# Spreading a finished batch's routing work over the next head pairs, in a block attention and top-1 expert kernel

## The chip, the cores and the metric

The kernel runs on one core of one Trainium2 chip. The metric is the device time in microseconds (us) from start to end of one execution, taken as the median over several runs. A profile is one execution of its own, with its own time.

## What is computed

Eight batches of eight heads with 576 positions and 64 dimensions go through attention with a block mask (blocks of 64 positions; a query sees its own block and the earlier ones). The rows of the result (4608 tokens of 512) then go through one of eight experts each, with two gates:

```python
scores = scale * np.matmul(q, k.transpose(0, 1, 3, 2))
scores = np.where(block_i >= block_j, scores, -1e9)
attn = softmax(scores)                       # over the keys
x = (attn @ v).transpose(0, 2, 1, 3).reshape(B * S, H * D)

e_idx = argmax(x @ w_gate)                   # one expert for each token
gate_w = softmax(x @ w_gate)[e_idx]
eom = sigmoid(x @ w_output_gate)
for e in range(E):
    out[e_idx == e] = gate_w * eom[:, e] * (relu(x @ w1[e]) @ w2[e])
```

## The kernel before, in words

The engines are called PE (TensorE), DVE (VectorE), ACT (ScalarE), POOL (GpSimd) and SP (SyncE, which issues most of the DMAs).

**Attention.** The outer loop runs over 32 pairs of heads, numbered 0 to 31, four pairs to a batch. The queries of a pair are cut into four tiles of 128 rows and a last one of 64. Pair p is worked on in three turns of the loop: in turn p its scores, in turn p+1 its flips, in turn p+2 its values. So one turn (`attend`) holds the scores of a pair, the flips of the pair before and the values of the pair before that.

- *Scores* (`softmax`) are a generator of four steps, here S1 to S4. Each fills a tile of `ps_s`, which is two banks of PSUM and of which there are two, so S3 takes the banks of S1, S4 those of S2, and the next pair's S1 and S2 those of S3 and S4. DVE takes the negated maxima (`nmx`, L374), ACT the exponentials (`pt`, L367; for S4 `plast`, L418). S1 does tiles 0 and 1, S2 tile 2, S3 tile 3, S4 the last. Ahead of S4 DVE also builds `qlast` (L393).
- *Flips* (`flip`), F1 to F4, transpose the exponentials on PE. F1 to F3 use `ps_f`, of which there is one (two banks), and ACT and DVE each copy one half out into `pT` (L445). F4 uses a bank of `ps_t` (L467, copied by ACT, L468).
- *Values* (`values`), V1 and V2, multiply the flipped exponentials with v (L481, L494) into a bank of `ps_t`. The result is copied to `xT` by ACT (L488, the first 512 positions) and by DVE (L498, the last 64).

`ps_t` has two banks, handed out in turn. Whoever asks for one waits until the tile that had it two requests earlier has been read.

**A finished batch's rest** is a generator, `finish_batch`, that is appended to the list `later` at the end of the turn that holds the values of the batch's last pair. In the attend loop each `t` is a tick, which moves every generator in `later` on by one yield; there are four ticks to a pair. The generator does, in this order: the sums of the last tile (`sumL`, a product on PE and two small copies), the reciprocals `rec`, the logits of both gates from `xT` in a part of 512 and one of 64 columns (L545, copied to `lgT`), their transposes (L561, L571) with a DVE product each into `lh`, a reduction of `lh` to the logits `L` (L577), the routing on small tiles (on POOL for the first five batches, on DVE for the others), a product that ranks the tokens of each expert (`pr`, L645 to L651), and five scatters of the tokens' slots into a table in DRAM. In between, `rows(t)` transposes one tile of `xT` back (four transposes, L517), DVE multiplies it with `rec` (L520), and one tick later `store` sends it to `x_d` in DRAM (L532).

**Order.** PE runs in the order in which the program issues its instructions within a turn. The other engines' queues are ordered by a planner of its own when the kernel is built, by costs and priorities; an instruction in `issue_after` stays behind a given one, and the maxima, for one, have a raised priority. The order of a turn is written in one string in `attend`. A dot in it calls `others`, which feeds SP and POOL: POOL splits q and k into two halves of 16 bits, SP turns them (`qk`, L164, a DMA transpose; from pair 8 on two pairs ahead, before that one), and SP loads q, k and v of later batches.

**The experts.** At pair 30 `load_first` is appended to `later`. In its first tick it finds the fullest expert, reads the table (`fetch_ids`, L889), gathers the first tokens from `x_d` (`xg`, L900) and loads that expert's first weights; from its sixth tick on it converts them. After pair 31 one more turn runs without scores, in which `stage_x` transposes the first gathered tokens (L999). Then the expert stage runs over 22 steps to the end.

Of the kernel before, what the change touches and what calls it, by code (L numbers as in the profile page):

```python
# [10 lines left out]
F32 = mybir.dt.float32  # L11
I32 = mybir.dt.int32
U32 = mybir.dt.uint32
AF = mybir.ActivationFunctionType
# [6 lines left out]
P = 128  # L21
# [5 lines left out]
def block_attention_top1_moe(  # L27
# [11 lines left out]
    nc = tc.nc  # L39
    B, H, S, D = q.shape  # L40
    NTOK, DM = out.shape
    E, _, FF = w1.shape
    NP = H // 2
# [4 lines left out]
    LAST = NT - 1  # L48
    S0 = P * LAST
# [23 lines left out]
    ps_t = tc.alloc_tile_pool(name="ps_t", bufs=2, space=PSUM)  # L73
    ps_f = tc.alloc_tile_pool(name="ps_f", bufs=1, space=PSUM)
    sbx = ctx.enter_context(tc.tile_pool(name="sbx", bufs=2))
# [62 lines left out]
    def queued():  # L138
        return tc.issue_after(last_turn[0].ins) if last_turn[0] else nullcontext()
# [57 lines left out]
    with tc.high_priority(offset=3000):  # L197
        ident16 = const.tile([P, P], F16, name="ident16")
        make_identity(nc, ident16)
        ident = const.tile([P, P], F32, name="ident")  # L200
# [301 lines left out]

    def finish_batch(b, sums, sumL, xT):

        pm = ps_t.tile([P, 512], F32, name="ps_t")
        nc.tensor.matmul(pm[0:64, 0:NP], ident[:, 64:128], sumL, start=True, stop=True)
        sv = sums[0:64, LAST].rearrange("p (g a) -> p a g", a=2)
        nc.scalar.copy(sv[:, 0], sumL[0:64])
        nc.vector.tensor_copy(sv[:, 1], pm[0:64, 0:NP])
        rec = small.tile([P, NT, H], F32, name="rec")  # L510

        def rows(t):

            r = ROWS[t]
            pm = ps_t.tile([P, 512], F32, name="ps_t")
            for g in range(NP):
                nc.tensor.transpose(pm[0:r, P * g:P * g + P], xT[:, g, Q0[t]:Q0[t] + r], ident)  # L517
            xn = sbx.tile([P, DM], F32, name="xn", bufs=NT)
            with tc.high_priority(offset=5):
                last_row[0] = nc.vector.tensor_tensor(  # L520
                    xn[0:r].rearrange("p (h d) -> p h d", d=D), pm[0:r].rearrange("p (h d) -> p h d", d=D),
                    rec[0:r, t].unsqueeze(2).broadcast_to([r, H, D]), ALU.mult,
                )
            held.append((x_d[b * S + Q0[t]:b * S + Q0[t] + r, :], xn[0:r]))
            if rush:
                store()

        def store():

            while held:  # L530
                with queued() if not rush else nullcontext():
                    nc.sync.dma_start(*held.pop())  # L532

        held, rush = [], b == B - 1
        if not rush:
            yield
        nc.scalar.activation(rec, sums, AF.Copy, bias=1e-9)
        if rush:
            nc.vector.reciprocal(rec, rec)

        lgT = sbx.tile([P, S], F32, name="lgT", bufs=1)
        for c0, c1 in ((0, 512), (512, 576)):
            pm = ps_t.tile([P, 512], F32, name="ps_t")
            for g in range(NP):
                nc.tensor.matmul(  # L545
                    pm[32 * g:32 * g + 32, 0:c1 - c0], wg_bd[:, g, :], xT[:, g, c0:c1],
                    start=True, stop=True, tile_position=(0, 32 * g),
                )
            nc.scalar.copy(lgT[:, c0:c1], pm[:, 0:c1 - c0])
            if not rush:  # L550
                yield
                if c0 == 0:
                    nc.vector.reciprocal(rec, rec)
        yield
        if not rush:
            rows(LAST)
            yield
            store()
        pm = ps_t.tile([P, 512], F32, name="ps_t")
        for t in range(LAST):  # L560
            nc.tensor.transpose(pm[:, P * t:P * t + P], lgT[:, Q0[t]:Q0[t] + P], ident)  # L561
# [8 lines left out]
        pm = ps_t.tile([P, 512], F32, name="ps_t")  # L570
# [14 lines left out]
        def on_pool(*ops):  # L585

            for op, args in ops:
                with behind() if slow else nullcontext():
                    ins = getattr(eng, op)(*args)
                if slow:  # L590
                    last_pool[0] = ins

        def after(last):
            return tc.issue_after(last[0].ins) if slow else nullcontext()

        def part(n):

            for x in range(n if slow else 0):
                yield

        def part_rows(t):

            if slow:
                rows(t)
                yield
                store()
# [3 lines left out]
        er = small.tile([P, NT], F32, name="er")  # L610
        oh = small.tile([P, NT, E], F16, name="oh")
        z = small.tile([P, NT, E], F32, name="z")
        yield from part(1)
        yield from part_rows(0)
        on_pool(
            ("tensor_tensor", (d, lg, mxb, ALU.subtract)),
            ("tensor_scalar", (eq, d, 0.0, None, ALU.is_equal)),
            ("tensor_tensor", (eq, eq, erev.unsqueeze(1).broadcast_to([P, NT, E]), ALU.mult)),
        )
        yield from part_rows(1)  # L620
        yield from part_rows(2)
        with after(last_max):
            nc.vector.tensor_reduce(er, eq, AX.X, ALU.max)
        yield from part_rows(3)
        erb = er.unsqueeze(2).broadcast_to([P, NT, E])
        on_pool(
            ("tensor_tensor", (eq, erb, erev.unsqueeze(1).broadcast_to([P, NT, E]), ALU.subtract)),
# [4 lines left out]
        if slow:  # L632
            with after(last_exp):
                nc.scalar.activation(d, d, AF.Exp)
        yield from part(2)
        if not slow:
            yield
            if not rush:
                for t in range(LAST):
                    rows(t)  # L640
                    yield
                    store()
# [28 lines left out]
        with after(last_max):  # L671
            nc.vector.tensor_reduce(zs, z, AX.X, ALU.add)
        yield from part(1)
        with after(last_exp):
            last_gate[0] = nc.scalar.activation(zs, zs, AF.Exp, scale=-1.0)
        yield from part(1)
# [464 lines left out]
    def attend(soft, extra=None):  # L1141

        nxt, flipped, valued = [], iter(()), iter(())
        if flips:
            hp, b, probs, sums, xT, vab = flips.pop()
            pT = sb.tile([P, 2, NPT], F32, name="pT")
            nxt = [(hp, b, pT, vab, sums, xT)]
            flipped = flip(probs, pT)
        if prods:
            hp, b, pT, vab, sums, xT = prods.pop()  # L1150
            valued = values(hp, pT, *vab, xT)
        else:
            hp = None
        def tick():
            for g in list(later):
                if next(g, later) is later:
                    later.remove(g)

        turns = iter(range(4))
        with tc.manual_schedule(engines=ENG):  # L1160
            for x in "S.F.SVFSV.FttSFtt.":
                if x == "S":
                    step(soft)
                elif x == "V":
                    step(valued)
                elif x == "F":
                    step(flipped)
                elif x == "t":
                    tick()
                elif extra is not None:  # L1170
                    extra(next(turns))

        if hp == NP - 1:
            later.append(finish_batch(b, *sums, xT))
        prods.extend(nxt)
# [4 lines left out]
    for p in range(NPR):  # L1180
        b, hp = divmod(p, NP)
        if hp == 0:
            sums = small.tile([P, NT, H], F32, name="sums", bufs=3), small.tile([P, NP], F32, name="sumL", bufs=3)
# [67 lines left out]
    ps_t = ctx.enter_context(tc.tile_pool(name="ps_y", bufs=4, space=PSUM, reuse_waits="tile"))  # L1251
    attend(iter(()), both_x)
    hp, b, pT, vab, sums, xT = prods.pop()
    ended = values(hp, pT, *vab, xT)
    rush = finish_batch(b, *sums, xT)
# [133 lines left out]
```

## Time and profile before

| | us |
|---|---|
| median of 3 runs | 743.06 |
| lowest and highest run | 740.52 to 744.53 |
| the profiled execution | 739.44 |
| its span, from the first to the last instruction | 737.8 |
| PE busy (share of the span) | 694.3 (94%) |
| DVE busy | 543.7 (74%) |
| ACT busy | 498.5 (68%) |
| POOL busy | 322.2 (44%) |

Busy times are those of the one profiled execution. Attention runs from the start to about 320 us, the experts from there to the end. Matmuls are pipelined and their ends are modelled, so a busy PE is not PE at its peak. A wait is the idle time of an engine just before an instruction, put down to the engine or DMA whose signal came last.

### The profile page before, as it was taken

Reading aid. Unit: us, or ns where it says so; the run is one execution under the profiler, and the core shown is the slowest. Engines: PE = TensorE matmul, PEld = TensorE weight load, DVE = VectorE, ACT = ScalarE, POOL = GpSimd, SP = SyncE. Lnnn points to the kernel's source line nnn. Section 1 sums busy time; section 2 is a strip of 40 time slices with the busy share of each in tenths; the row PEclk is TensorE's granted clock in tenths of the full one; section 3 lists DMA queues with packets and bytes.
Section 4 is the critical chain, followed back from the end, with each engine's and each line's share of the span. In section 5 each row is a group of like instructions: output and inputs, shape, how many; then the busy total and the mean of one; then the engine's idle time right before and its main releaser. Section 6 shows DMA issues by size and latency. Waiting matters only on the chain. (4 is left out here: it accounts for less than half of the span.)

```text
span 737.8 us, 21153 instructions
## 1 busy us (share of the span) xinstructions
PE 694.3 (94%) x8298; PEld 492.7 (67%) x8298; DVE 543.7 (74%) x948; ACT 498.5 (68%) x1097; POOL 322.2 (44%) x407
## 2 busy tenths in 40 slices
PE   5899899999999898989989999999999999999994
PEld 4666666767677676657568666876577676767861
DVE  6887878888797879798757558955588667858830
ACT  5888777878687886873357558765576577658630
POOL 4365378685758583246366523422233124211011
PEclk9999999999999999999999999999999999999998
DMA  7699897999989898176645796987999999686601
GB/s 199 143 198 224 181 219 132 205 151 177 203 181 178 155 152 173 55 270 137 186 143 131 221 281 190 298 88 255 250 306 361 290 325 342 220 232 191 240 31 46
DMA packets 235997, 146.85 MB, mean 199 GB/s; under 512 B 187120, under 2 KB 203568, under 8 KB 235888
## 3 DMA queue, kind: packets, MB, share of 16 engines
q1 hardware_dynamic: 227136, 125.85, 70.2%
q0 software_dynamic: 8208, 19.29, 8.5%
q8 instruction: 67, 1.10, 0.7%
q14 instruction: 42, 0.34, 0.1%
q10 hardware_dynamic: 544, 0.26, 0.1%
HBM read 126.43 MB, written 19.34 MB: 198 GB/s over the span
## 5 line engine op out<-in xcount | busy, mean ns | idle before, releaser
L1055 PEld LDWEIGHTS <-w1b 128*128 128x128 f16 (+1 forms) x2208 | 176.3, 98 | 26.3 <-issue 4.9
L1055 PE MATMUL ps_s<-xt,w1b 128*128 128x256 f16 (+5 forms) x1920 | 175.3, 253 | 0.3 <-DVE w1b L933 0.2
L1090 PE MATMUL ps_t<-w2b,hh 128*128 128x512 f16 (+1 forms) x560 | 166.5, 379 | 0.0
L933 DVE TENSOR_TENSOR w2b<-w2f,w2b 128x1024 bf16<-128x1024 f32 x80 | 92.9, 1220 | 88.1 <-ACT w2b L931 88.1
L374 DVE TENSOR_REDUCE nmx<-ps_s 128x1 f32<-128x512 f32 (+4 forms) x224 | 130.0, 617 | 11.4 <-PE ps_s L363 6.8
L367 ACT ACTIVATE pt<-ps_s,nmx 128x256 f32<-128x256 f32 (+3 forms) x256 | 131.9, 534 | 8.8 <-DVE nmx L374 8.7
L1098 POOL DMA_INDIRECT out_dram<-ys,ids x38 | 45.3, 1192 | 174.6 <-ACT ys L1097 95.9
L1090 PE MATMUL ps_t<-w2b,hl 128*128 128x512 f16 x280 | 106.1, 379 | 0.0
L1097 ACT ACTIVATE ys<-ps_t,ids 128x512 f32<-128x512 f32 (+1 forms) x38 | 26.0, 685 | 103.7 <-PE ps_t L1090 77.2
L933 DVE TENSOR_TENSOR w1b<-w1f,w1b 128x1024 bf16<-128x1024 f32 x80 | 93.1, 1218 | 3.8 <-ACT w1b L931 3.6
L1090 PEld LDWEIGHTS <-hh 128*128 128x128 f16 x560 | 54.3, 98 | 61.7
L355 PE MATMUL ps_s<-qk 64*128 64x256 f16 (+1 forms) x1152 | 73.8, 252 | 11.5 <-ACT plast L418 3.7
L445 DVE COPY pT<-ps_f 128x512 f32<-128x512 f32 x93 | 63.8, 686 | 28.0 <-PE ps_f L442 25.9
L481 PE MATMUL ps_t<-pT,vv 128*64 128x256 f32 (+3 forms) x512 | 83.0, 445 | 0.4 <-DVE lh L572 0.4
L931 ACT CAST w1b<-w1f 128x1024 f16<-128x1024 f32 x80 | 78.5, 1045 | 7.0 <-DMA w1f<-in_moe_w_dram 6.9
L931 ACT CAST w2b<-w2f 128x1024 f16<-128x1024 f32 x80 | 77.9, 1043 | 1.0 <-DMA w2f<-in_moe_w_dram 0.7
L900 POOL DMA_INDIRECT xg<-x_d,ids x38 | 62.5, 1646 | 32.8 <-DMA ids<-tab_d 7.0
L355 PEld LDWEIGHTS <-qk 64*128 64x128 f16 x1152 | 49.9, 94 | 23.5 <-issue 14.9
L445 ACT COPY pT<-ps_f 128x512 f32<-128x512 f32 x93 | 55.3, 595 | 10.0 <-PE ps_f L442 8.9
L442 PEld LDWEIGHTS ps_f<-ident,pt 64*128 64x128 f32 x1116 | 42.2, 138 | 25.6 <-issue 12.3
L1063 ACT ACTIVATE hh<-ps_s 128x1024 f16<-128x1024 f32 (+2 forms) x46 | 38.9, 845 | 29.5 <-PE ps_s L1055 27.5
L442 PE MATMUL ps_f<-ident,pt 64*128 64x64 f32 x1116 | 54.1, 229 | 4.2 <-DVE pT L445 2.3
(220 smaller groups left out, 1029.3 us busy)
## 6 DMA issues: line engine op xcount, KB each, us to landing
w1f<-in_moe_w_dram SPq DMA_DIRECT2D x80, 512.0 KB
w2f<-in_moe_w_dram SPq DMA_DIRECT2D x80, 512.0 KB
vv<-in_v_dram SPq DMA_DIRECT2D x64, 128.0 KB
x_d<-xn SPq DMA_DIRECT2D x32, 256.0 KB
natk<-in_k_dram SPq DMA_DIRECT2D x14, 512.0 KB
natq<-in_q_dram SPq DMA_DIRECT2D x28, 256.0 KB
hh<-in_moe_w_dram SPq DMA_DIRECT2D x4, 512.0 KB
hl<-in_moe_w_dram SPq DMA_DIRECT2D x4, 512.0 KB
```

What stands on the lines that cost most here:

```text
L355: nc.tensor.matmul(ps[:, ab, c:c + m], qk[rows, cq, P * t:P * t + P], cols(qk[rows, ck], x, kind), start=(i == 0), stop=(i == 2 and c + m ...
L367: last_exp[0] = nc.scalar.activation(probs[t][:, ab], ps[:, ab, c0:c0 + n], AF.Exp, bias=nmx[:, t, ab:ab + 1], accum_out=sums[:, t, 2 * hp ...
L374: last_max[0] = nc.vector.tensor_reduce(o, x, AX.X, ALU.max, negate=True)
L442: nc.tensor.transpose(ps[:, h, 64 * i:64 * i + 64], src[rows], ident[rows, rows])
L445: copy(to[:, h], ps[:, h].rearrange("p (s c) -> p s c", c=P))
L481: nc.tensor.matmul(pa[o, P * j:S0].rearrange("p (t h n) -> p t h n", h=2, n=64), vv[:, j, a0 + ab], pT[:, :, x:x + P * m].rearrange("p h ( ...
L900: nc.gpsimd.indirect_dma_start(out=xg[i % NXG][:, h], out_offset=None, in_=x_d[0:nx, :], in_offset=IOA(ap=ids[i][:, h, 0:1].bitcast(U32), ...
L931: nc.scalar.copy(hi, src)
L933: eng.tensor_tensor(lo, src, hi, ALU.subtract)
L1055: nc.tensor.matmul(ph[:, f4].rearrange("p (h n) -> p h n", n=w), wv[:, cc, f, :], xv[:, cc, :, 0:w], start=(k == 0), stop=(k == 3 * KD - 1))
L1090: nc.tensor.matmul(py, hv[:, f, h], wv[:, f, :], start=(k == 0), stop=(k == 3 * KF - 1))
L1098: nc.gpsimd.indirect_dma_start(out=out, out_offset=IOA(ap=ids[i][0:r, h, 0:1].bitcast(U32), axis=0), in_=ys[0:r], in_offset=None, bounds_c ...
```

## The change

Three things change; what is computed stays the same.

- The order of a turn: before `S.F.SVFSV.FttSFtt.`, after `S.tF.VSFSV.FttSFt.`. V1 moves from behind S2 to ahead of it. Of the four ticks of a pair, the one at the very end moves to the place behind S1, ahead of F1; two stay between F3 and S4, one behind F4.
- The short part of the logits (64 columns) is taken in the first tick, in the same PSUM tile as the sums; the long part in the second.
- The tiles of `rows` are laid out differently over the ticks. For the first five batches: before, the last tile in tick 5, then 0 to 3 in ticks 8 to 11, the ranking in tick 14 and the scatters from tick 20 on; after, the transposes of the logits in ticks 5 and 6, the last tile and tile 0 in ticks 9 and 10, tiles 1 and 2 in ticks 13 and 14, the ranking in tick 16, tile 3 in tick 17, and the scatters from tick 23 on. The later batches (but the very last) take the last tile behind the routing instead of ahead of it.

```diff
@@ finish_batch @@
-        pm = ps_t.tile([P, 512], F32, name="ps_t")
-        nc.tensor.matmul(pm[0:64, 0:NP], ident[:, 64:128], sumL, start=True, stop=True)
-        sv = sums[0:64, LAST].rearrange("p (g a) -> p a g", a=2)
-        nc.scalar.copy(sv[:, 0], sumL[0:64])
-        nc.vector.tensor_copy(sv[:, 1], pm[0:64, 0:NP])
         rec = small.tile([P, NT, H], F32, name="rec")
...
-        held, rush = [], b == B - 1
-        if not rush:
-            yield
-        nc.scalar.activation(rec, sums, AF.Copy, bias=1e-9)
-        if rush:
-            nc.vector.reciprocal(rec, rec)
-
         lgT = sbx.tile([P, S], F32, name="lgT", bufs=1)
-        for c0, c1 in ((0, 512), (512, 576)):
-            pm = ps_t.tile([P, 512], F32, name="ps_t")
+
+        def logits(c0, c1, pm):
             for g in range(NP):
                 nc.tensor.matmul(
                     pm[32 * g:32 * g + 32, 0:c1 - c0], wg_bd[:, g, :], xT[:, g, c0:c1],
                     start=True, stop=True, tile_position=(0, 32 * g),
                 )
             nc.scalar.copy(lgT[:, c0:c1], pm[:, 0:c1 - c0])
-            if not rush:
-                yield
-                if c0 == 0:
-                    nc.vector.reciprocal(rec, rec)
-        yield
-        if not rush:
-            rows(LAST)
+
+        held, rush = [], b == B - 1
+        pm = ps_t.tile([P, 512], F32, name="ps_t")
+        nc.tensor.matmul(pm[0:64, P:P + NP], ident[:, 64:128], sumL, start=True, stop=True)
+        sv = sums[0:64, LAST].rearrange("p (g a) -> p a g", a=2)
+        nc.scalar.copy(sv[:, 0], sumL[0:64])
+        nc.vector.tensor_copy(sv[:, 1], pm[0:64, P:P + NP])
+        if rush:
+            nc.scalar.activation(rec, sums, AF.Copy, bias=1e-9)
+            nc.vector.reciprocal(rec, rec)
+            logits(0, S0, ps_t.tile([P, 512], F32, name="ps_t"))
+            logits(S0, S, ps_t.tile([P, 512], F32, name="ps_t"))
             yield
-            store()
+        else:
+            logits(S0, S, pm)
+            yield
+            nc.scalar.activation(rec, sums, AF.Copy, bias=1e-9)
+            logits(0, S0, ps_t.tile([P, 512], F32, name="ps_t"))
+            yield
+            nc.vector.reciprocal(rec, rec)
+            yield
+            yield
...
-        yield from part(1)
-        yield from part_rows(0)
+        yield from part(3)
         on_pool(
...
-        yield from part_rows(1)
-        yield from part_rows(2)
+        yield from part_rows(LAST)
+        yield from part_rows(0)
         with after(last_max):
             nc.vector.tensor_reduce(er, eq, AX.X, ALU.max)
-        yield from part_rows(3)
+        yield from part(1)
...
-        yield from part(2)
+        yield from part(1)
+        yield from part_rows(1)
+        yield from part_rows(2)
+        yield from part(1)
         if not slow:
             yield
             if not rush:
-                for t in range(LAST):
+                for t in (LAST, *range(LAST)):
...
         yield from part(1)
+        yield from part_rows(3)
         with after(last_exp):
             last_gate[0] = nc.scalar.activation(zs, zs, AF.Exp, scale=-1.0)
@@ attend @@
-            for x in "S.F.SVFSV.FttSFtt.":
+            for x in "S.tF.VSFSV.FttSFt.":
```

## Rows read from the trace of the kernel before

**Rows 1.** Busy time by stretch: start, length, engines, granted clock, DMA share, GB/s.

```profile
100.00:200.00 100.00, 95.36 (x1549) 68.93 (x1547) 82.47 (x179) 79.68 (x251) 75.10 (x114) 1.00 0.97 179
200.00:300.00 100.00, 93.82 (x1538) 68.52 (x1539) 85.32 (x194) 78.17 (x248) 62.25 (x94) 1.00 0.83 161
500.00:600.00 100.00, 100.00 (x887) 69.37 (x885) 66.98 (x66) 64.91 (x79) 26.79 (x24) 1.00 0.99 299
```

**Rows 2.** Waits of PE, 30 to 380 us: total, times, longest us.

```profile
PE ps_s L355 <- ACT plast L418: 3.7, 9, 0.7
PE ps_t L999 <- DMA xg<-x_d,ids: 2.6, 1, 2.6
PE ps_s L355 <- DMA qk<-sp: 2.5, 2, 1.4
PE ps_f L442 <- DVE pT L445: 2.3, 5, 0.5
...
PE ps_s L355 <- ACT pt L367: 1.8, 7, 0.3
...
PE ps_t L545 <- DVE xT L498: 1.1, 1, 1.1
PE ps_t L517 <- ACT xT L488: 0.7, 1, 0.7
PE ps_t L571 <- DVE lh L562: 0.6, 1, 0.6
PE ps_t L545 <- DVE sums L509: 0.5, 1, 0.5
PE ps_f L442 <- DVE d L589: 0.5, 1, 0.5
```

**Rows 3.** Timeline of PE: start, us, line, what, count, [idle before].

```profile
42.79 0.92 PE L412 MATMUL ps_s<-qk,qlast 128*128 128x256 f16 x9
...
45.42 0.67 PE L355 MATMUL ps_s<-qk 64*128 64x256 f16 x12 [0.28 <-ACT plast L418]
...
46.05 1.73 PE L481 MATMUL ps_t<-pT,vv 128*64 128x512 f32 x8
47.71 0.58 PE L442 MATMUL ps_f<-ident,pt 64*128 64x64 f32 x12
...
51.05 0.92 PE L412 MATMUL ps_s<-qk,qlast 128*128 128x256 f16 x9
...
110.86 0.92 PE L412 MATMUL ps_s<-qk,qlast 128*128 128x256 f16 x9
...
149.22 0.92 PE L412 MATMUL ps_s<-qk,qlast 128*128 128x256 f16 x9
```

**Rows 4.** Timeline of DVE, 122 to 126 us.

```profile
122.46 0.69 DVE L520 TENSOR_TENSOR xn<-ps_t,rec 128x512 f32<-128x512 f32 x1 [0.36 <-PE ps_t L517]
123.07 1.23 DVE L577 TENSOR_REDUCE L<-lh 128x80 f32<-128x640 f32 x1
...
125.25 0.69 DVE L445 COPY pT<-ps_f 128x512 f32<-128x512 f32 x1
```

**Rows 5.** Timelines of PE's weight loads (PEld) and of SP around waits for qk.

```profile
92.38 0.11 PEld L355 LDWEIGHTS <-qk 64*128 64x128 f16 x3 [1.95 <-DMA qk<-sp]
...
257.99 0.17 PEld L355 LDWEIGHTS <-qk 64*128 64x128 f16 x6 [1.59 <-DMA qk<-sp]
...
247.75 0.57 SPq L532 DMA_DIRECT2D x_d<-xn  x1
...
249.97 4.45 SPq L164 DMA_TRANSPOSE qk<-sp  x1
```

**Rows 6.** Timelines of PE, DVE and POOL at the first table read.

```profile
305.81 0.18 PE L719 MATMUL ps_t<-run_cnt,ones 128*128 128x8 f16 x1
...
306.38 0.15 DVE L721 COPY cnt<-ps_t 128x8 f32<-128x8 f32 x1
...
310.74 0.78 POOL L889 DMA_DIRECT2D ids<-tab_d  x1 [10.30 <-DVE nmx L374]
```

## Prediction

> **What bounds the kernel now.** I read the engine shares first, then the busy time by stretch, then who waits for whom, then the timelines of TensorE (PE), VectorE (DVE), ScalarE (ACT) and SyncE (SP). By stretch, PE is busy for 95.4% and 93.8% of the attention loop (100 to 200 and 200 to 300 us) and for 100% of the expert stage, at a granted clock of 1.00 in all three [rows 1]. So the expert stage starts and ends as much earlier as attention does, and what the change can win is PE's idle time in attention.
>
> That time is small and named. Between 30 and 380 us PE waits 3.7 us (9 times) for ACT's exponential of the last tile (plast), 2.3 us for the DVE half of a flip's copy and 0.5 us more under another DVE name, 1.8 us for the exponentials pt, 2.5 us for turned q and k (qk), 2.6 us for the first gathered tokens (xg), and four times 0.5 to 1.1 us for a bank of ps_t [rows 2].
>
> A pair of heads without any rest of a batch in it takes 51.05 - 42.79 = 8.26 us from one S4 to the next, of which 0.28 us is a wait for plast [rows 3]: 7.98 us of PE work. DVE and ACT are busy for 82.5% and 79.7% from 100 to 200 us [rows 1], rest included, so they have room on average. The waits come from work that arrives in a lump.
>
> **The change, part by part.** The sum is made against the profiled execution, 739.4 us (span 737.8), which is 3.6 us under the median of 743.06; I carry the difference over to the median.
>
> *V1 ahead of S2.* S2 fills the pair of ps_s banks that the S4 before it filled, so it waits for the exponential of plast. Before, F4, two ticks, S1 and F1 lie between them; now V1 does too. V1 takes 47.71 - 46.05 = 1.66 us [rows 3], and no wait for plast is above 0.7 us [rows 2]. All 3.7 us should go. What it costs: this 1.66 us no longer lies between S2 and F2, S3, F3. I laid such a pair out by hand with the start-to-start times of the 20 rows from 42.79 to 51.05 [rows 3]: S1 at 0, F1 0.56, V1 1.24, S2 2.90, F2 3.53, S3 4.07, V2 4.85, F3 6.23, S4 6.87, F4 7.63, next S1 7.98. DVE then has S2's maxima, F2's copy, qlast and S3's maxima in one run, about 3.4 us from 3.7 on; ACT ends S3's second exponential at about 7.95, and the next S1, which takes that bank pair, starts at 7.98. It just fits. With a product of rows or logits between F3 and S4, as in nearly every later pair, it fits with room. I take a cost of 0; the work that hides it is that product, and without it the cost is 0.1 to 0.5 us a pair.
>
> *The rest spread out.* PE's work for a finished batch stays the same; it only moves. What changes is DVE's queue. Before, rows(LAST), both lh products, rows(0) and the 1.23 us reduction of lh fall between F3 of a batch's second pair and F1 of its third; S1's maxima queue behind the reduction, so that F1's copy starts only at 125.25 [rows 4], and F2 on PE waits 0.46 us and S3 0.25 us. In all that is 2.3 + 0.5 us for F2, and for S3 six times 0.25 of the 1.8: 4.3 us [rows 2]. After it, the rows are gone from there, but the reduction stands right behind F3's copy, so S4's maximum, its exponential and the next S1's maxima come up to 1.2 us later. Between nothing left and all left I take half: 2.1 us won.
>
> *Banks of ps_t.* The 512-column logits wait 1.1 + 0.5 us for small copies on DVE, L571 0.6 and a row's transposes 0.7: 2.9 us [rows 2]. The logits now run a tick after the 64-column ones, in the bank of a tile long read; I take 2.0 as won. New is the first tick of a batch's first pair: it holds rows(3) of the batch before, sumL and the short logits, which are two tiles of ps_t, and V1, only F1 later, takes the bank of rows(3). Its product (0.69 us, as at 122.46 [rows 4]) stands behind S1's maxima on DVE. I put 0.3 us on each of six batches, -1.8; the bounds are 0 and 0.7 each.
>
> *DMA issues.* The number of transfers is unchanged. On SP, the store of rows(LAST), 0.57 us, stands just ahead of the turn of qk that is needed soonest (issued at 249.97, landed at 257.99 [rows 5]); it moves behind it. The stores of rows(1) to rows(3) move among the next loads of q and k. POOL's scatters into the table come three ticks later; nothing reads the table before the last batches are in. Two waits for qk (its weight loads stand at 92.38 and 257.99 [rows 5]) shrink by 0.6 us each, and grow by what PE comes early: the 0.84 us won in pairs 3 to 5 falls into an earlier wait for qk at 61.6, pair 8's 0.35 into the one at 92.4, and one batch's gain, 1.0, into the one at 258. Net -1.0 us.
>
> *The start of the experts.* load_first takes the first tick of pair 30, which moves from behind F3 (its product ran at 305.81 [rows 6]) to behind S1, about 298.3: 7.5 us earlier. The table read at 310.74 [rows 6] and the gather behind it come earlier with it, and PE's 2.6 us wait for xg should go. Its dozen small DVE operations (the first, 0.15 us, at 306.38 [rows 6], so some 1.8 us) now stand ahead of F1's copy; I take 0.5 us as lost. Net 2.1.
>
> Sum: 3.7 + 2.1 + 2.0 - 1.8 - 1.0 + 2.1 = 7.1 us won. 739.4 becomes 732.3, and the median 743.1 becomes 736.0.
>
> **A rule weighed.** The same short gaps come back on PE in every batch [rows 2]. The Trainium skill, page "Perfetto Trace Analysis", section "Optimization Strategy", says that a gap which repeats on the engine that should be full can mean that SBUF or PSUM has no room for the next tile. By that rule a new order would only move the gaps, as the change adds no bank, and the sum would be what the expert start alone gives. The sum above goes by the rows: the waits end on a named copy or exponential that is late by less than V1 takes.
>
> **The rivals.** *Transfers set the pace (0.20).* From 100 to 200 us the DMA share is 0.97 [rows 1], and a turn that takes 4.45 us to issue lands 3.6 us after that [rows 5]. If qk can't come sooner, all that is won before 258 us goes into waits for qk, and only pairs 28 to 31 and the expert start gain: about 3 us, 740. Against it: from 200 to 300 us the share is 0.83 [rows 1], and only 2.5 us of waits name qk now [rows 2]. The Trainium skill, page "Perfetto Trace Analysis", section What "DMA-bound" means, counts a kernel as bound by the DMA sequencer where the issuing engine's track is solid DMA; by that rule this rival is the case. The trace agrees only for part of the loop.
>
> *The lump moves onto S3 (0.11): slower.* The place is DVE's run from S2's maxima to S3's. If one more operation of 0.69 us [rows 4], a copy or a row's product, is queued ahead of S3's maxima, the next S1 waits some 0.5 us in about 26 pairs: 13 us, less the 7 won: 749. It decides from the point where S3's second exponential ends after S1 could start, 7.95 against 7.98 us above. Against it: rest lies between F3 and S4 in nearly every pair and adds room there.
>
> *Everything goes (0.13).* The named waits but those for qk, 13.8 us in all [rows 2], go, less the 0.84 of pairs 3 to 5, and nothing new comes: 730.1.
>
> *It moves the gaps and wins nothing (0.08).* The expert start alone gains its 2.1 us: 741.
>
> **How the numbers follow.** The forecast has the rest, 0.48: 736.0, its own range 732 to 740. The range of 729.0 to 744.5 takes in everything gone, the paced transfers and a small loss; it leaves out the slower rival and little else. A change under 0.5% (3.7 us) can't be told from none here. Faster by more: most of the forecast (0.46), everything gone (0.13), a third of the paced transfers and of the moved gaps (0.08): 0.67. Same: the rest of these, 0.22. Slower: the lump, 0.11.
>
> **What would show it.** Right: no wait of S2 for plast; four pairs of a batch in about 37.4 us from S4 to S4, where it is 149.22 - 110.86 = 38.36 [rows 3]; no wait for xg ahead of the first stage_x; the table read more than 12 us earlier than before. Wrong: PE waits for qk in more than two pairs, above all in a batch's first pair; S1 waits for pt in most pairs; V1 waits for the product of rows(3) by more than 0.7 us; F2 of a batch's third pair still waits 0.46 us.

## The result, and the profile after

The changed kernel takes 752.44 us (751.2 to 756.46, five runs) where the kernel before takes 744.53 us beside it (740.52 to 746.56, five runs): a ratio of 1.0138, 95% interval 1.0106 to 1.0171. It is slower by 7.9 us between the medians and by some 10 us by the ratio, where 736.0 was forecast in a range of 729.0 to 744.5. The profiled execution is one of 752.44 us (span 750.8).

Busy time by stretch, which answers to [rows 1]:

```profile
100.00:200.00 100.00, 93.14 (x1505) 65.88 (x1504) 79.07 (x175) 76.74 (x245) 67.00 (x105) 1.00 0.91 185
200.00:300.00 100.00, 92.58 (x1486) 66.11 (x1484) 83.04 (x188) 75.94 (x240) 64.06 (x95) 1.00 0.79 157
500.00:600.00 100.00, 99.74 (x885) 69.70 (x888) 68.18 (x66) 63.75 (x77) 26.63 (x23) 1.00 0.90 260
```

PE is less busy in the loop (93.1% and 92.6%), and ACT, DVE and the DMA share are all lower too: nothing is fuller, PE only waits more. These rows show what for (the waits of PE from 30 to 380 us, as [rows 2]; the new lines are L533 for the logits, L512 for the transposes of rows, L544 for the copy of the sums):

```profile
PE ps_f L442 <- ACT pT L445: 6.8, 10, 1.5
PE ps_t L533 <- DVE sums L544: 6.1, 6, 1.0
PE ps_t L512 <- ACT pT L468: 1.9, 1, 1.9
PE ps_t L494 <- issue: 1.9, 3, 1.1
...
PE ps_f L442 <- DVE er L623: 1.2, 1, 1.2
PE ps_s L355 <- ACT pt L367: 1.2, 3, 0.8
PE ps_t L533 <- issue: 1.1, 1, 1.1
...
PE ps_f L442 <- DVE se L590: 0.7, 1, 0.7
```

No wait for plast is left, none for qk and none for xg. In their place stand two new groups: F2 waits 6.8 us for ACT's half of F1's copy, and the short logits wait 7.2 us (6.1 and 1.1) for the copy of the sums. (A line with "issue" names no releaser; the 1.1 us end behind that copy too, in the first batch.) The S4 of [rows 3] show where it counts:

```profile
45.49 0.92 PE L412 MATMUL ps_s<-qk,qlast 128*128 128x256 f16 x9
...
53.43 0.92 PE L412 MATMUL ps_s<-qk,qlast 128*128 128x256 f16 x9
...
111.57 0.92 PE L412 MATMUL ps_s<-qk,qlast 128*128 128x256 f16 x9
...
152.41 0.92 PE L412 MATMUL ps_s<-qk,qlast 128*128 128x256 f16 x9
```

A pair without rest takes 53.43 - 45.49 = 7.94 us, 0.32 less than before, as worked out. But four pairs with rest take 152.41 - 111.57 = 40.84 us, where before had 38.36 and 37.4 was forecast.

*The short logits.* The timeline of all engines, at the first tick of a batch's first pair (behind S1, ahead of F1):

```profile
143.28 1.01 DVE L374 TENSOR_REDUCE nmx<-ps_s 128x2 f32<-128x512 f32 x2
...
143.70 0.28 PE L541 MATMUL ps_t<-sumL,ident 128*64 128x4 f32 x2
...
144.21 0.68 DVE L515 TENSOR_TENSOR xn<-ps_t,rec 128x512 f32<-128x512 f32 x1
...
144.81 0.14 DVE L544 COPY sums<-ps_t 64x4 f32<-64x4 f32 x1
...
145.01 0.32 PE L533 MATMUL ps_t<-xT,wg_bd 128*32 128x64 f32 x8 [1.02 <-DVE sums L544]
```

PE puts out the sums, DVE has first to finish S1's maxima and the product of rows(3), then copies the sums, and only then do the short logits run. The first and the last of the seven batches have no product of rows(3) in this tick; there the copy stands behind the maxima alone, and the wait is as long (1.08 and 1.03 us). The tick holds a round trip from PE to DVE and back, and F1, V1 and S2 are queued behind it.

*F1's copy.* The same view in the batch's third pair:

```profile
125.19 0.47 ACT L367 ACTIVATE pt<-ps_s,nmx 128x256 f32<-128x256 f32 x1 [1.10 <-DVE mx L581]
...
125.72 0.67 DVE L445 COPY pT<-ps_f 128x512 f32<-128x512 f32 x1
...
126.45 0.37 ACT L367 ACTIVATE pt<-ps_s,nmx 128x128 f32<-128x128 f32 x1
...
126.79 0.60 ACT L445 COPY pT<-ps_f 128x512 f32<-128x512 f32 x1
...
127.44 0.59 PE L442 MATMUL ps_f<-ident,pt 64*128 64x64 f32 x12 [1.50 <-ACT pT L445]
```

ACT runs all four exponentials of S1 (125.19 to 126.8) and only then its half of F1's copy. Before, ACT's queue held the copy ahead of them (the kernel before, in the same pair):

```profile
123.48 0.59 ACT L445 COPY pT<-ps_f 128x512 f32<-128x512 f32 x1 [0.49 <-PE ps_f L442]
...
125.27 0.47 ACT L367 ACTIVATE pt<-ps_s,nmx 128x256 f32<-128x256 f32 x1 [1.20 <-DVE nmx L374]
```

ACT and DVE are ordered by the planner; that it places the exponentials first because the tick ahead of F1 makes F1 late on PE is an inference. DVE's half is ready at 126.4 and not what F2 waits for.

### The profile page after: what moved, and what is told of

Read it like the earlier page. It is cut to its first block, busy times and chain, and to the rows that moved or that the text cites. A ratio compares the mean times of both kernels' runs of the same rounds, so it can differ in the third digit from the quotient of the medians.

```text
span 750.8 us, 21165 instructions
## 1 busy us (share of the span) xinstructions
PE 702.3 (94%) x8277; PEld 494.9 (66%) x8298; DVE 541.8 (72%) x948; ACT 499.0 (66%) x1097; POOL 316.0 (42%) x407
## 5 line engine op out<-in xcount | busy, mean ns | idle before, releaser
L1094 PE MATMUL ps_t<-w2b,hh 128*128 128x512 f16 (+1 forms) x539 | 162.1, 379 | 0.0
L481 PE MATMUL ps_t<-pT,vv 128*64 128x256 f32 (+3 forms) x512 | 85.7, 455 | 0.2 <-issue 0.2
L355 PE MATMUL ps_s<-qk 64*128 64x256 f16 (+1 forms) x1152 | 72.2, 256 | 2.4 <-ACT pt L367 1.2
L904 POOL DMA_INDIRECT xg<-x_d,ids x38 | 54.3, 1429 | 34.4 <-DVE w1b L937 10.6
L355 PEld LDWEIGHTS <-qk 64*128 64x128 f16 x1152 | 46.7, 95 | 29.7 <-issue 25.8
L700 POOL DMA_INDIRECT tab_d<-idg,sli x40 | 41.9, 1048 | 42.3 <-DVE sli L668 34.5
```

What stands on the lines that cost most here:

```text
L355: nc.tensor.matmul(ps[:, ab, c:c + m], qk[rows, cq, P * t:P * t + P], cols(qk[rows, ck], x, kind), start=(i == 0), stop=(i == 2 and c + m ...
L481: nc.tensor.matmul(pa[o, P * j:S0].rearrange("p (t h n) -> p t h n", h=2, n=64), vv[:, j, a0 + ab], pT[:, :, x:x + P * m].rearrange("p h ( ...
L904: nc.gpsimd.indirect_dma_start(out=xg[i % NXG][:, h], out_offset=None, in_=x_d[0:nx, :], in_offset=IOA(ap=ids[i][:, h, 0:1].bitcast(U32), ...
L1094: nc.tensor.matmul(py, hv[:, f, h], wv[:, f, :], start=(k == 0), stop=(k == 3 * KF - 1))
```

## The experiments

Each ratio is against runs of the kernel before on the same chip; brackets hold the 95% interval. The ratio is not the quotient of the two medians and can differ from that by up to 0.3%. A profile is one execution, so waits and times from S4 to S4 are those of one run. Times from S4 to S4 are differences of such rows as above: "the loop" is S4 of pair 2 to S4 of pair 28, "the end" pair 28 to pair 31.

**What belongs to the kernel before anyway.** Two more profiles of it, unchanged.

> The kernel before once more, unchanged, for a second profile. In all five profiles with a changed order, also with V1 alone moved, TensorE stands nearly still for some 3 us in V2 of pair 29, VectorE and ScalarE with it, and pair 28 to pair 29 takes 11.9 to 12.9 us from S4 to S4, where the first profile of the kernel before has 9.5 and no such stop. Theory 'the new order brings the stop': the second profile has none either, 9.5 us within 0.3. Theory 'the stop comes by chance and the first profile was without': it is there, 11.5 to 13 us, and its time is 3 us above the first.

743.8 us, span 742.2, 4.4 us above the first profile. The stop is there: pair 28 to 29 takes 12.92 us. So it does not come with the new order. PE's timeline there, and busy time by stretch:

```profile
295.42 0.34 PE L494 MATMUL ps_t<-pT,vv 128*64 128x64 f32 x4
296.19 0.22 PE L494 MATMUL ps_t<-pT,vv 128*64 128x64 f32 x1 [0.44 <-issue]
296.90 0.34 PE L494 MATMUL ps_t<-pT,vv 128*64 128x64 f32 x4 [0.50 <-issue]
298.32 0.55 PE L494 MATMUL ps_t<-pT,vv 128*64 128x64 f32 x6 [1.07 <-issue]
```

```profile
15.00:20.00 5.00, 4.31 (x39) 3.16 (x41) 2.78 (x7) 2.54 (x8) 0.00 (x0) 0.51 1.04 255
290.00:300.00 10.00, 7.65 (x118) 5.44 (x113) 5.80 (x15) 5.69 (x20) 6.57 (x7) 0.92 0.47 103
```

The start at a granted clock of 0.51 (15 to 20 us), which the changed kernel's profile shows too (0.75), is also the kernel before's own. Against this profile the changed one, 8.6 us longer in span, loses 0.7 us up to pair 2, 6.8 in the loop (257.07 against 250.26), 2.8 in the end (35.97 against 33.21), and wins 1.7 behind it. Neither this profile nor the third has a wait for xg; the first had 2.6 us.

**Which of the two waits costs what.** First, the short logits in a tile of their own:

```diff
-            logits(S0, S, pm)
+            logits(S0, S, ps_t.tile([P, 512], F32, name="ps_t"))
```

> The changed kernel, but with the short logits in a PSUM tile of their own instead of the tile of the sums. In the changed kernel the short logits wait 1.02 us on TensorE in nearly every batch, 7.2 us in all, and the trace names VectorE's copy of the sums. Theory 'shared tile': the wait is there because the two share a tile; with a tile of their own it goes, and the time falls by about 7 us, to 745. Theory 'place of the tick': the tick stands behind tile 0 and 1's scores, so whatever it needs back from VectorE queues behind those maxima (1.01 us) and behind the product of rows(3) (0.68 us); with two banks in ps_t the short logits then take the bank of rows(3) and wait for that product, which ends at the same moment; the wait stays near 1.0 us under another name and the time stays at 752, within 2 us.

750.34 us, 1.0095 [1.0058, 1.0132]. The interval overlaps the changed kernel's. The waits of L533 come to 6.1 us, in five batches instead of seven. One of the five (the same view as above):

```profile
143.98 0.68 DVE L515 TENSOR_TENSOR xn<-ps_t,rec 128x512 f32<-128x512 f32 x1
...
144.58 0.14 DVE L544 COPY sums<-ps_t 64x4 f32<-64x4 f32 x1
...
144.72 0.32 PE L533 MATMUL ps_t<-xT,wg_bd 128*32 128x64 f32 x8 [0.96 <-DVE sums L544]
```

The product and the copy end together, so this row alone can't tell the bank of rows(3) from the sums. The batches without rows(3) can. The last of them, in the changed kernel:

```profile
310.38 0.14 DVE L544 COPY sums<-ps_t 64x4 f32<-64x4 f32 x1
...
310.58 0.32 PE L533 MATMUL ps_t<-xT,wg_bd 128*32 128x64 f32 x8 [1.03 <-DVE sums L544]
```

and with a tile of their own:

```profile
313.53 0.32 PE L533 MATMUL ps_t<-xT,wg_bd 128*32 128x64 f32 x8
...
314.44 0.14 DVE L544 COPY sums<-ps_t 64x4 f32<-64x4 f32 x1
```

Here the short logits run ahead of the copy and wait for nothing. So the shared tile is what they wait for where no product of rows(3) stands in the tick, and a tile of their own takes that wait away. In the five other batches it takes the bank of rows(3) instead, and the wait stays: 0.96 us in four of them, 2.29 in one. Each theory holds for a part.

Then F1's copy with a higher priority:

```diff
+            with tc.high_priority(offset=60) if c0 == 3 else nullcontext():
                 one, other = (
```

> The changed kernel with a higher priority for the two halves of F1's copy as the only change: in ScalarE's queue F1's copy then stands behind one of the four exponentials of tiles 0 and 1, not behind all four. Theory 'order of ScalarE's queue': the 6.8 us in which F2 waits for this copy fall below 2, and the time falls by 4 to 6 us, a ratio of 1.006 to 1.009 where the changed kernel has 1.0138. Rival 'the lump moves': the exponentials come later instead, TensorE waits for pt or plast ahead of S3 or the next S1, and the ratio stays at 1.012 to 1.015. The 7.2 us of waits of the short logits are in it unchanged.

750.72 us, 1.0093 [1.0058, 1.0127]: the waits for this copy fall from 6.8 to 0.4 us and the loop from 257.07 to 252.35. The ratio lies just above the range of the first theory, and its interval reaches into that of the second; by the time alone this run can't be told from own_tile (1.0095). What speaks for the first theory is the wait that goes and the 4.7 us in the loop. The waits of the short logits are all there (6.1 and 1.1).

Then the short logits one tick later, ahead of the long ones:

```diff
-            logits(S0, S, pm)
             yield
             nc.scalar.activation(rec, sums, AF.Copy, bias=1e-9)
+            logits(S0, S, ps_t.tile([P, 512], F32, name="ps_t"))
             logits(0, S0, ...
```

> The changed kernel with the short logits in the second tick (ahead of the long ones, in a tile of their own) instead of the first; the first tick keeps only the sums. Theory 'round trip inside the tick': the 7.2 us in which the short logits wait for VectorE's copy of the sums go, F2's waits for F1's copy stay near 6 us, and the ratio falls from 1.0138 to 1.004 to 1.007. Rival 'the wait moves': V1 or the logits wait for the same copies, and the ratio stays at 1.010 or above.

741.67 us on a chip where before takes 735.46: 1.0084 [1.0053, 1.0115], between the two theories. The 7.2 us are gone but for 2.8: 1.6 in which the logits now wait for xT and 1.2 in which V1 waits for the sums. F2 waits 5.0 us for F1's copy, a little less than expected. New are 5.8 us of waits for qk, in four places, where the changed kernel has none.

Then the tick behind V1, which takes away both at once:

```diff
-            for x in "S.tF.VSFSV.FttSFt.":
+            for x in "S.F.VtSFSV.FttSFt.":
```

> The changed kernel with its first tick behind V1 instead of ahead of F1 (S.F.VtSFSV.FttSFt.); nothing else differs. Theory 'place of the tick': both of the changed kernel's new waits go, the 7.2 us of the short logits and most of the 6.8 us that F2 waits for ScalarE's half of F1's copy, because ScalarE's queue then holds F1's copy ahead of the four exponentials of tiles 0 and 1 again; about 13 us won, 739 to 742, below the kernel before. Theory 'the end decides': the waits in the loop are made up for elsewhere and the 13 us are lost in the last pairs and at the start of the experts, where TensorE idles and its clock drops to 0.66; then it stays at 747 or above.

747.24 us, 1.0067 [1.0039, 1.0095]. Half of the loss goes; F2's waits for ACT's copy fall to 0.7 us, the short logits' to 1.5 (waits of PE):

```profile
PE ps_s L355 <- DMA qk<-sp: 6.7, 4, 2.4
PE ps_t L541 <- DVE xn L515: 3.9, 5, 0.8
...
PE ps_f L442 <- ACT pT L445: 0.7, 3, 0.3
```

It doesn't come out below before: the sums wait 3.9 us for the bank of the rows(3) product and PE waits 6.7 us for qk, in four pairs.

**The place of the tick alone, in the old layout.** The turn's string is the only edit to the kernel before, first with the tick ahead of F1, then with it ahead of F2:

```diff
-            for x in "S.F.SVFSV.FttSFtt.":
+            for x in "S.tF.SVFSV.FttSFt.":
...
-            for x in "S.F.SVFSV.FttSFtt.":
+            for x in "S.F.SVtFSV.FttSFt.":
```

> The kernel before with the tick of the pair's end moved ahead of F1 as the only change (S.tF.SVFSV.FttSFt.). Theory 'place of the tick': a tick ahead of F1 is enough to lose time: in one pair of each batch ScalarE's queue holds F1's copy behind the four exponentials (1.6 us), and F2 waits 0.5 to 1.5 us for it there; 3 to 8 us slower, a ratio of 1.004 to 1.011. The sums and the short logits are in different ticks here, so their wait is not there. Rival 'only the new layout of the rest costs': the ratio is 1.000 within 0.003.

750.77 us, 1.0129 [1.0084, 1.0173], four runs: above the range of the first theory, and not for its reason alone. Waits of PE:

```profile
PE ps_t L571 <- DVE xT L498: 2.9, 3, 1.0
PE ps_t L467 <- ACT lgT L549: 2.9, 7, 0.5
PE ps_f L442 <- ACT pT L445: 2.4, 5, 0.9
```

F2 waits only 2.4 us for ACT's half of F1's copy. The rest of the loss is spread over other waits, of the logits' transposes and of rows' transposes, which stand in a tick; no run parts them.

> The kernel before with the tick of the pair's end moved behind V1, ahead of F2 (S.F.SVtFSV.FttSFt.); V1 stays behind tile 2's scores. It differs from the run tick_f1 (ratio 1.013) only in where that tick stands. Theory 'place ahead of F1': the loss is that place, not the step from four ticks at the pair's end to one in its middle; the ratio is 0.998 to 1.004. Rival 'any tick in the middle costs': 1.009 or above.

734.68 us where before takes 735.46: 0.9982 [0.9952, 1.0012]. Two kernels that differ only in where one of four ticks stands are 1.5% apart (1.0129 / 0.9982, each against before on its own chip). Ahead of F1, that tick alone costs as much as the whole change, but by a different set of waits. (F4's 2.9 us for lgT aren't part of it: tick_v1_old has 2.3 of them and loses nothing.)

**V1's move.** Alone on the kernel before; taken back in the new layout (beside tick_v1); and added to the harmless tick on the kernel before (beside tick_v1_old):

```diff
-            for x in "S.F.SVFSV.FttSFtt.":
+            for x in "S.F.VSFSV.FttSFtt.":
...
-            for x in "S.F.VtSFSV.FttSFt.":
+            for x in "S.F.SVtFSV.FttSFt.":
...
-            for x in "S.F.SVtFSV.FttSFt.":
+            for x in "S.F.VtSFSV.FttSFt.":
```

> The kernel before with V1 ahead of tile 2's scores as the only change (S.F.VSFSV.FttSFtt.). Theory of the prediction: the 3.7 us of waits for plast go and nothing comes in their place: 740 to 741 where the kernel before has 744.5, a ratio of 0.995. Rival (gaps only move): the waits come back in front of F2, S3 or the next pair's tile 0 and 1, and the ratio is 1.000 within 0.003.

744.85 us, 1.0025 [0.9996, 1.0053], as the rival has it. No wait for plast is left. PE waits 2.7 us for pt, where the three profiles of before have 1.8, 1.1 and 1.8, and 1.5 us of the logits' transposes (L561) for xT are new.

> The new layout of the rest, its first tick behind V1, and V1 back behind tile 2's scores (S.F.SVtFSV.FttSFt.); it differs from the run tick_v1 only in the order of V1 and S2. Theory of the prediction: V1's move is worth 3.7 us in any layout, so this one is slower than tick_v1 by that, a ratio of 1.011 to 1.013 where tick_v1 has 1.0067, with 7 to 10 waits for plast. Theory 'V1's move wins nothing': the ratio is 1.004 to 1.009, as in the run with V1 alone moved.

749.0 us, 1.0063 [1.0036, 1.0090], where tick_v1 has 1.0067; as the second theory has it; it waits 6.6 us for plast, 21 times, and never for qk, where tick_v1 waits 6.7.

> The kernel before (its own layout of the rest) with V1 ahead of tile 2's scores and the tick of the pair's end behind V1 (S.F.VtSFSV.FttSFt.). It differs from tick_v1_old (ratio 0.998) only in V1 and S2, and from the changed kernel in the place of that tick and in the layout. Theory 'both moves are harmless, none wins': 0.997 to 1.003. Theory of the prediction (V1's move wins 3.7 us once nothing else is in its way): 0.991 to 0.995.

733.85 us, 0.9969 [0.9938, 1.0000], where tick_v1_old has 0.9982. Three comparisons give V1's move +0.25%, 0.04% and -0.13%: nothing that can be told from none, although the waits for plast come and go with it. (The second and the third are between two chips, and the third doesn't shut out the forecast gain of 0.5%.) In v1_tick_old PE waits 5.5 us for qk, where tick_v1_old has 3.3 and before, on the chip of v1_tick_old, 0.5.

**The new layout, repaired.** On top of tick_v1, rows(3) one tick earlier:

```diff
-        yield from part(1)
         yield from part_rows(3)
+        yield from part(1)
```

> As tick_v1, but rows(3) one tick earlier, with the ranking at the end of the pair, so that the tick of the sums holds no product. In tick_v1 the sums wait 0.78 us in five batches for the bank of that product, 3.9 us. Theory 'banks of ps_t': these 3.9 us go and the ratio falls from 1.0067 to 1.000 to 1.003. Rival 'transfers set the pace': TensorE then waits for qk instead (6.7 us in four pairs in tick_v1), and the ratio stays above 1.005.

746.66 us, 1.0030 [0.9996, 1.0064]: the 3.9 us are gone. In its profile, which is of its fastest run (740.86 us), four pairs take 37.90, 37.53, 37.71 and 37.53 us, close to the 37.4 forecast (before_again: 38.66 to 38.86). Then two row tiles of batches 5 and 6 ahead of the transposes of their logits:

```diff
+            if b >= B - 3:
+                for t in (LAST, 0):
+                    rows(t)
+                    yield
+                    store()
...
-                for t in (LAST, *range(LAST)):
+                for t in range(1, LAST):
```

> As tick_v1_r3e, but the two batches that are finished in a hurry (5 and 6) take two of their row tiles ahead of the transposes of the logits, as the last one was before, so that the burst of small routing operations on VectorE (3 us) falls into the tick behind F4, as in the kernel before, and not behind F3. Theory 'the burst': in tick_v1_r3e F2 waits 1.9 us for it in pair 28 and V1 of the end turn 3.9 us for a row's product in its midst; both go, the end from pair 28 to 31 falls from 35.3 to about 33 us, and the ratio from 1.003 to 0.996 to 0.999: below the kernel before. Rival 'the end is bound otherwise' (turned weights, gathers, the clock): the ratio stays at 1.002 or above.

736.95 us where before takes 735.46: 1.0004 [0.9971, 1.0037]. All of the loss is gone, and nothing is won. The end falls from 35.35 to 29.34 us, but that chip shows no stop in pair 29, and short_later, on the same chip without this edit, has an end of 28.07 us: the shorter end isn't shown to be the edit's. The two waits that it was made for do change: the 1.9 us of F2 are gone, and in place of the 3.9 us V1 of the end turn waits 2.4. The loops of tick_v1_r3e and fast_old are 244.95 and 244.29 us, where the two profiles of before so far have 252.43 and 250.26. For the question of where the shorter loop goes, a profile of each on one chip:

> The kernel before, unchanged, for a profile on the same chip as the next two runs. Theory 'the loop is won, the end gives it back': pairs 2 to 28 take 250 to 252.5 us, as in its two other profiles, and the end from pair 28 to 31 takes 30 to 33. Rival 'the gain was one between chips': on a chip where transfers come sooner its pairs 2 to 28 take 247 us or less, and the repaired layout wins nothing there.

> The repaired layout (run fast_old) once more, unchanged, for a second profile beside one of the kernel before on the same chip. Theory 'the loop is won': pairs 2 to 28 take 244 to 246 us, 5 us or more below the kernel before on this chip. Rival 'waits for qk take it': it waits 6 us or more for qk, and pairs 2 to 28 take as long as those of the kernel before, within 2 us.

Spans of 731.8 and 735.9 us, loops of 248.88 and 251.65: here the loop isn't won, though fast_old is the same kernel, and before's loop lies between the two theories of its run. PE of the repaired layout is 2.3 us ahead at pair 8 (87.91 against 90.23) and 3.0 us behind at pair 9. Its PE timeline and busy time by stretch, and then those of the kernel before:

```profile
91.92 0.50 PE L355 MATMUL ps_s<-qk 64*128 64x128 f16 x6 [2.86 <-DMA qk<-sp]
...
94.01 3.25 PE L481 MATMUL ps_t<-pT,vv 128*64 128x512 f32 x8
```

```profile
92.50:95.00 2.50, 2.50 (x28) 1.64 (x26) 1.62 (x3) 0.88 (x3) 2.36 (x5) 0.50 1.13 239
```

```profile
91.93 0.28 PE L355 MATMUL ps_s<-qk 64*128 64x128 f16 x3 [0.54 <-DMA qk<-sp]
```

```profile
92.50:95.00 2.50, 2.50 (x50) 1.97 (x50) 2.16 (x4) 1.60 (x6) 2.20 (x7) 1.00 1.01 198
```

The turned q and k come at 91.9 us in both, although PE is earlier in one. The wait eats the 2.3 us, and behind it the clock is granted at its level of 1.2 GHz (0.50), V1 takes 3.25 us instead of 1.72, and another 3.0 us are lost. The rival of that run (waits for qk take it) fits this stretch, but not its own figures: from 30 to 380 us the waits for qk add up to 4.9 us, not 6 or more, and the loops differ by 2.8, not within 2. And fast_old has no wait at this place: it is at pair 8 at 88.81 and at pair 9 at 97.67. So whether the repaired layout's lead is lost here differs between executions of one kernel.

**The end.** In v1_tick_old V1 of the last turn waits for a row's product that is queued among the small operations of the routing (the line names one of them, eq, which ends 0.1 us after that product):

```profile
316.87 3.25 PE L481 MATMUL ps_t<-pT,vv 128*64 128x512 f32 x8 [3.97 <-DVE eq L589]
```

One run takes this product ahead of the burst, one does the same for the short product of the logits in fast_old:

```diff
-            with tc.high_priority(offset=5):
+            with tc.high_priority(offset=5 if b < B - 3 else 60):
```

```diff
+        with tc.high_priority(offset=60) if b >= B - 3 else nullcontext():
             nc.vector.tensor_tensor(lh[0:64, LAST], ...
```

> As v1_tick_old, with a higher priority for the products of rows of the last three batches, so that in the end turn the one whose bank V1 takes stands ahead of the routing burst in VectorE's queue. In v1_tick_old V1 waits 3.97 us there and then runs 3.25 instead of 1.72 us at a granted clock of 0.50. Theory 'the end gives it back': both go, 4 to 5.5 us, and the ratio falls from 0.997 to 0.990 to 0.993: clearly faster than both kernels. Rival 'the start of the experts is bound by the gathers and the turned weights': TensorE waits there instead, and the ratio stays at 0.995 to 0.999.

744.84 us where before takes 742.56: 1.0030 [1.0015, 1.0045], outside both theories. V1's wait falls to 1.3 us and V1 takes 1.73 us again, yet nothing is won: PE waits for what now comes later (waits of PE):

```profile
PE ps_s L1055 <- DVE xl L1001: 3.4, 1, 3.4
PE ps_t L645 <- DVE oh L589: 2.9, 1, 2.9
...
PE ps_t L481 <- DVE w1b L973: 1.3, 1, 1.3
```

> As fast_old (the new layout with its three repairs), with a higher priority for the short product of the logits in the last three batches, which V1 of the end turn waits for (2.44 us). Theory 'the new layout wins nothing even when repaired': the ratio stays at 0.997 to 1.002, because what the loop gains goes into waits for qk and the clock behind them. Rival 'its gain is only hidden by the end': 0.993 to 0.996, as much under the kernel before as its loop is shorter.

744.55 us, 1.0016 [0.9985, 1.0047]: as the first theory has it. V1's wait of 2.4 us is gone, and PE waits 6.0 us for qk, in six places. No version tried is faster than the kernel before by more than can be told from none; v1_tick_old comes nearest.

## Why the prediction was wrong

Two steps failed. The rest of a batch, spread out, was put at a gain because only DVE's queue was followed and not ACT's; and the first tick ahead of F1 was priced for one product, not for the round trip from PE to DVE and back inside it. A third, V1's move, was right in its mechanism and worth nothing measurable.

*V1 ahead of S2, +3.7.* The mechanism was right, its worth was not: the waits for plast go (0 left), a bare pair takes 7.94 us, and the time doesn't fall. Other waits stand in its place, not the same in each run: 2.7 us for pt in v1_only, 1.8 for F1's copy and 5.5 for qk in v1_tick_old, 6.7 for qk in tick_v1. The step that failed is the one from "this wait ends" to "the end comes earlier by as much", with a cost of 0.

*The rest spread out, +2.1.* This has the wrong sign. Only DVE's queue was followed through the third pair. ACT's was never looked at, and there F1's copy fell behind four exponentials: F2's waits went from 2.8 to 8.7 us, 6.8 of them for this copy. f1_first shows it: with the copy raised in the queue this wait falls to 0.4 us and the loop by 4.7. tick_v1 shows that the place of the tick brings it (0.7 us left). In the old layout the same place costs as much time (tick_f1), but only 2.4 us of it by this wait.

*Banks of ps_t, +2.0 and -1.8.* The place was right (the first tick of a batch's first pair), the size and the waiter were not. The price was 0.3 us, at most 0.7, for V1 in six batches; measured are 1.0 us for the short logits in seven, 7.2 us. The bound failed because it counted the product of rows(3) and not the copy of the sums, which is queued behind S1's maxima and, where there is one, behind that product, and which PE needs inside the tick. own_tile shows it (with a tile of their own the short logits wait for nothing in the two batches without rows(3), and for that bank in the other five), and short_later, where the 7.2 us shrink to 2.8. The price for the bank of rows(3) itself was too small too: in tick_v1 the sums wait 3.9 us for it, and in tick_v1_r3e those are gone.

*DMA issues, -1.0.* There is no wait for qk in this profile, probably because PE is late: own_tile, 2.6 us ahead of it at pair 5 (58.94 against 61.49), waits 2.4 us for qk right behind, and never again once it is late itself. In the versions with the tick behind V1 the waits for qk go from none (v1_old) to 6.7 us (tick_v1): transfers do set the pace in some pairs, which was given 0.20, and the price was short by what the clock adds.

*The start of the experts, +2.1.* The wait for xg is gone, but two of three profiles of before don't have it either: the term rested on one execution. The table read comes at 315.28, 4.5 us later than in [rows 6], since PE is 12 us behind by then. Not foreseen was that the routing burst of batches 5 and 6 moves from behind F4 to behind F3, where F2 waits 1.2 and 0.7 us for it, and that V1 of the last turn runs at the lower clock (0.67 from 335 to 340 us; 2.83 us).

*The rivals.* The slower one (0.11) named the wrong queue: S1 waits for pt three times, 1.2 us in all, not in 26 pairs. *Everything goes* and *wins nothing* both needed that no new wait comes, and two came.

*The rule weighed* (the Trainium skill, page "Perfetto Trace Analysis", section "Optimization Strategy") says that a gap which repeats can mean too little SBUF or PSUM for the next tile. The prediction drew from it that the gaps would only move, and so they did: from plast to F1's copy and the sums, and in rows_first from V1 to the routing. But the time it gave, 741, was too low, since the new gaps are longer than the old ones. In own_tile five of the waits are for a bank; that room is what lacks isn't shown, as no run adds one.

*The carry of 3.6 us* from the first profile to the median was of the right size: before_again takes 4.4 us more than the first profile, 3.4 of them from pair 28 to 29, where the stop is.

*Open.* The steps 1.0067, 1.0030 and 1.0004 come from three chips, and their intervals overlap; the step from 1.0138 to 1.0067 is clear of both intervals, and so is the whole way. Which wait takes what V1's move gives wasn't settled, nor what makes up all of tick_f1's loss, nor what decides whether qk comes in time.

## What to carry to other kernels

Ahead of a move on one engine's hand-written order, read every other engine's queue at the new place: an operation that moves a little on PE can fall behind a whole group on ACT. A step whose result PE needs back at once must not stand where DVE has just been given other work. And take a second profile of the kernel before: a wait that only one of them shows is no term of a sum.

## What the runs showed of the hardware

A wait can cost twice: 2.86 us for qk were followed by a granted clock of 0.50 and some 3.0 us more. Not every wait does: 1.81 us for qk at the same place in v1_tick_old left V1 behind it at 1.72 us. And in pair 29 PE issues V2 in steps of 0.7 us for about 3 us while VectorE and ScalarE wait, in 11 of the 18 profiles: in all ten taken on three of the chips, in none of the six on two others, whatever the order of the work (of the first two profiles, whose chip isn't on record, the changed kernel's has it); what it waits for, no row names, and no run tested it.
